# The bias of a Sin activation: a number in the instruction in place of a column in SBUF

## The chip, the cores and the metric

The kernel runs on one core of one Trainium2 chip. The metric is device microseconds of that core for one execution, and the median of a few runs is compared. The engines of the core are TensorE (PE in the profile, with its weight loads as PEld), VectorE (DVE), ScalarE (ACT), GpSimd (POOL) and SyncE (SP).

## The reference, cut to what matters

```python
# q, k, v: (4, 12480, 128); agents: (4, 49, 128); w_in: (128, 2048); w_out: (2048, 128), all fp32
def sm(a, b):                      # softmax of scaled scores over the last axis
    ...
a2k = sm(agents, k);  agent_v = a2k @ v          # 49 agents gather from 12480 keys
q2a = sm(q, agents);  x = (q2a @ agent_v).reshape(49920, 128)
h = x @ w_in                                      # 49920 x 2048
g = h * np.cos(h)
out = g @ w_out
```

Most of the arithmetic is the last three lines: for each of 49,920 tokens, 2,048 hidden values h, their cosine, and a second product.

## The kernel before, in words

**Tiling.** A batch has 13 groups of 960 tokens, so there are 52 groups. A group is worked in two halves of 480 tokens, and a half in 8 steps; a step handles 2 of the 16 blocks of 128 hidden units for 480 tokens. That makes 16 steps in a group and 832 in all. The projected agents times w_in are kept as `a`, so h comes straight from the softmax weights `pT` of the query: `ph = a' @ pT` (L520, two matmuls of 480 columns into a PSUM tile of two banks).

**A step.** After the two matmuls into `ph`, ScalarE computes cos(h) as Sin(h + pi/2) from `ph` into the SBUF tile `c` (L523), and VectorE computes r = (c - 1) * h from `c` and `ph` (L525). Four steps later TensorE multiplies r by w_out and accumulates into the PSUM tile `one` (L542). The missing "+ h" is added as two small matmuls at the end of each half (L538, L539). Then ScalarE copies the half's result from `one` to SBUF as `osb` (L544), and a DMA writes it out. `ph` has 3 buffers, `c` 3, `r` 6, and `one` 2: a step's matmuls into `ph` can start only when VectorE has read the `ph` of three steps earlier.

```python
cos = sb.tile([P, 2, CH], F32, name="c", bufs=3)
nc.scalar.activation(cos, h, AF.Sin, bias=half_pi, scale=1.0)
r = rs[n] = sb.tile([P, 2, CH], F32R, name="r", bufs=6)
nc.vector.scalar_tensor_tensor(r, cos, 1.0, h, op0=ALU.subtract, op1=ALU.mult)
```

**Work between the steps.** A plan written out by hand gives most steps one more piece of work: for the next batch, the agents' scores over the keys (L93 on TensorE, copied by ScalarE at L171), their exponentials (L214), and their product with v (L232); for the queries, scores (L93), maxima (L342), exponentials (L353), sums (L357) and weights, which TensorE turns (L372), ScalarE copies to SBUF as `p` (L374) and GpSimd splits into the rows of `pT` (L377, L378). The last batch has no next one, so from about 1000 us on only the steps, the `osb` copies and the turning of weights are left. Ahead of the steps, until about 85 us, the first batch's agents and the weights are prepared.

**Order.** The instructions of each engine stand in one queue and are executed in that order. The queues are written by a planner in the library: it takes instructions in the order of the program unless its own estimate of times says that a later one is ready sooner; exponentials are pinned to their place.

**The column.** `half_pi` is a tile of 128 x 1 fp32 in SBUF, filled with pi/2 by GpSimd at the start (L66). Sin reads it as bias at L523; a 1 x 1 Sin that brings the Sin table in early reads one element of it as its input (L386). A branch for large h (L564 on) has a Sin with the same bias (L625); it is executed only if the data ask for it. `HALF_PI` is the Python number.

Of the kernel before, what the change touches and what calls it, by code (L numbers as in the profile page):

```python
# [13 lines left out]
AF = mybir.ActivationFunctionType  # L14
# [12 lines left out]
HALF_PI = math.pi / 2  # L27
# [14 lines left out]
def agent_attention_cos_ffn(ctx, tc, qT, kT, v, agT, w_in, w_out, outT):  # L42
    nc = tc.nc
# [21 lines left out]
    half_pi = const.tile([P, 1], F32, name="half_pi")  # L65
# [21 lines left out]
    def scores(sb, src, b, ps):  # L87

        xt = sb.tile([P, GRP], F32, name="xt", bufs=3)
        load(xt, src)  # L90
        ps = ps[:TT, :GT * NA].rearrange("p (t a) -> p t a", a=NA)
        for t in range(GT):
            nc.tensor.matmul(ps[:, t, :], xt[:, t * TT:(t + 1) * TT], ag[:, b, :], start=True, stop=True)  # L93
        return ps
# [204 lines left out]
    with ExitStack() as pools:  # L299
# [4 lines left out]
        def small():  # L304
            return ps_1.tile([P, 512], F32, name="one")
# [206 lines left out]
        for n in range(NSTEP + LAG):  # L512
            pinned[0] = n < NP
            if n < NSTEP:
                q, c, i = n // STEP, n // NP % NCH, n % NP
                ai = a[q // NG % 2]
                ph = ps_h.tile([P, 2, 512], F32, name="ph")
                for j in range(2):
                    f = slice((2 * i + j) * P, (2 * i + j + 1) * P)
                    nc.tensor.matmul(ph[:, j, :CH], ai[:, f], pTs[q % 3][:, c], start=True, stop=True)  # L520
                h = ph[:, :, :CH]
                cos = sb.tile([P, 2, CH], F32, name="c", bufs=3)
                nc.scalar.activation(cos, h, AF.Sin, bias=half_pi, scale=1.0)  # L523
                r = rs[n] = sb.tile([P, 2, CH], F32R, name="r", bufs=6)
                nc.vector.scalar_tensor_tensor(r, cos, 1.0, h, op0=ALU.subtract, op1=ALU.mult)  # L525
            plan.run(n)
            m = n - LAG
            if m < 0:
                continue
            q, c, i = m // STEP, m // NP % NCH, m % NP  # L530
            if i == 0:
                if c == 0:
                    osb = sb.tile([P, GRP], F32, name="osb")
                po = small()[:, :CH]
            r = rs.pop(m)
            if i == NP - 1:
                k = q // NG % 2
                nc.tensor.matmul(po, b1[k], pTs[q % 3][:, c], start=False, stop=False)  # L538
                nc.tensor.matmul(po, b2[k], pTs[q % 3][:, c], start=False, stop=False)  # L539
            for j in range(2):  # L540
                f = 2 * i + j
                nc.tensor.matmul(po, w1[:, f, :], r[:, j, :], start=(f == 0), stop=(f == NF - 1))  # L542
            if i == NP - 1:
                nc.scalar.copy(osb[:, c * CH:(c + 1) * CH], po)  # L544
                at = q * GRP
                if q == NQ - 1:
                    nc.sync.dma_start(outT[:, at + c * CH:at + (c + 1) * CH], osb[:, c * CH:(c + 1) * CH])
                elif c == NCH - 1:
                    nc.sync.dma_start(outT[:, at:at + GRP], osb)
# [14 lines left out]
    with tc.If(far):  # L564
        with ExitStack() as pools:
# [19 lines left out]
            def group(b, src, dst):  # L585
                ps = scores(sb, src, b, small())
                mx = sb.tile([TT, GT], F32, name="mx2")
                nc.vector.reduce_max(mx, ps, axis=AX.X)
                e = sb.tile([TT, GT, NA], F32, name="e")
                nc.vector.tensor_sub(e, ps, mx.unsqueeze(2).to_broadcast([TT, GT, NA]))  # L590
                nc.scalar.activation(e, e, AF.Exp, scale=SC)
                rz = sb.tile([TT, GT], F32, name="rz2")
                nc.vector.reduce_sum(rz, e, axis=AX.X)
                nc.vector.tensor_scalar_add(rz, rz, EPS)
                nc.vector.reciprocal(rz, rz)
                nc.gpsimd.tensor_mul(p.rearrange("p t (h a) -> p h t a", h=2)[:, :, :, :NA],
                                     e.rearrange("p (h t) a -> p h t a", h=2),
                                     rz.rearrange("p (h t) -> p h t", h=2).unsqueeze(3).to_broadcast([TT, 2, HT, NA]))
                pt = small()
                for t in range(HT):  # L600
                    nc.tensor.transpose(pt[:KR, t * TT:(t + 1) * TT], p[:, t, :KR], ident[:TT, :TT])
                for c in range(NCH):
                    own, other = half_rows[c], half_rows[1 - c]
                    nc.scalar.copy(pT[own, c], pt[own, :CH])
                    nc.vector.tensor_sub(pT[other, c], pt[own, :CH], pT[own, c].bitcast(F32))
                osb = sb.tile([P, GRP], F32, name="osb")
                for c in range(NCH):
                    po = small()[:, :CH]
                    for i in range(NP):
                        ph = ps_h.tile([P, 2, 512], F32, name="ph")  # L610
                        for j in range(2):
                            f = slice((2 * i + j) * P, (2 * i + j + 1) * P)
                            nc.tensor.matmul(ph[:, j, :CH], a1[:, f], pT[:, c], start=True, stop=False)
                            nc.tensor.matmul(ph[:, j, :CH], a2[:, f], pT[:, c], start=False, stop=True)
                        h = ph[:, :, :CH]

                        k = sb.tile([P, 2, CH], F32, name="k", bufs=1)
                        nc.vector.tensor_scalar(k, h, 0.5 / math.pi, 0.25, op0=ALU.mult, op1=ALU.add)
                        nc.vector.tensor_scalar(k, k, ROUND, ROUND, op0=ALU.add, op1=ALU.subtract)
                        r = sb.tile([P, 2, CH], F32, name="r", bufs=1)  # L620
                        nc.vector.scalar_tensor_tensor(r, k, -TWO_PI_A, h, op0=ALU.mult, op1=ALU.add)
                        nc.vector.scalar_tensor_tensor(r, k, -TWO_PI_B, r, op0=ALU.mult, op1=ALU.add)
                        nc.vector.tensor_scalar(r, r, -4.7123885, 1.5707960, op0=ALU.max, op1=ALU.min)
                        cos = sb.tile([P, 2, CH], F32, name="c")
                        nc.scalar.activation(cos, r, AF.Sin, bias=half_pi, scale=1.0)  # L625
                        y = sb.tile([P, 2, CH], F32, name="g")
                        nc.vector.tensor_mul(y, h, cos)
                        g1 = sb.tile([P, 2, CH], F32R, name="g1")
                        nc.scalar.copy(g1, y)
                        g2 = sb.tile([P, 2, CH], F32R, name="g2")  # L630
                        nc.vector.tensor_sub(g2, y, g1.bitcast(F32))
                        for j in range(2):
                            f = 2 * i + j
                            nc.tensor.matmul(po, w1[:, f, :], g1[:, j, :], start=(f == 0), stop=False)
                            nc.tensor.matmul(po, w2[:, f, :], g1[:, j, :], start=False, stop=False)
                            nc.tensor.matmul(po, w1[:, f, :], g2[:, j, :], start=False, stop=(f == NF - 1))
                    nc.scalar.copy(osb[:, c * CH:(c + 1) * CH], po)
                nc.sync.dma_start(dst, osb)
# [55 lines left out]
```

## Time and profile before

| what | value |
|---|---|
| median of 3 runs | 1284.95 us (1282.61 to 1286.02) |
| span of the profiled execution | 1283.9 us |
| instructions | 17193 |
| granted TensorE clock, mean | 0.978 |
| PE, DVE, ACT, POOL busy | 93%, 85%, 78%, 24% |

The span runs from the first to the last instruction of one profiled execution, for which no other time of its own was taken. It is 1.05 us under the median of the runs, and within their spread. Shares of busy time are means over parts of the kernel that differ.

### The profile page before, as it was taken

The numbers are of one execution on the slowest core, as the hardware profiler recorded it, in microseconds if no ns is written. First come the engines' busy times: TensorE is split into PE (matmuls) and PEld (weight loads), VectorE is DVE, ScalarE is ACT, GpSimd is POOL, SyncE is SP. The second block draws the span as 40 slices with busy tenths as digits, with TensorE's granted clock in tenths as the row PEclk, the third lists the DMA queues.
The fourth block names the chain that finished last, engine by engine and source line by source line (L and its number), as shares of the span: only waits on it lengthen the run. The fifth ranks groups of instructions, "written<-read, shape, count | busy, mean of one in ns | idle before, by whom it ended". The sixth has DMA issues, their size and how long they took to land.

```text
span 1283.9 us, 17193 instructions
## 1 busy us (share of the span) xinstructions
PE 1188.2 (93%) x6349; PEld 955.3 (74%) x6349; DVE 1087.6 (85%) x1214; ACT 1005.6 (78%) x1115; POOL 313.8 (24%) x341
## 2 busy tenths in 40 slices
PE   8799899996999999969999999996999999999997
PEld 8777787775987887758966788775986666666664
DVE  5878778887779888878799988787789999999997
ACT  2347778667779887676799988667789999999997
POOL 1201221415213115133132121415133122222220
PEclk9989999998999999999999999998999999999999
DMA  8953333331440342324400133331500000000000
GB/s 301 247 153 111 92 108 108 93 109 61 109 108 31 108 131 70 108 77 108 133 22 31 54 116 93 108 93 31 136 19 32 31 16 31 31 31 16 31 31 34
DMA packets 31016, 107.72 MB, mean 84 GB/s; under 512 B 3436, under 2 KB 3820, under 8 KB 30924
## 3 DMA queue, kind: packets, MB, share of 16 engines
q1 hardware_dynamic: 30924, 106.54, 27.3%
q8 instruction: 52, 0.85, 0.3%
q14 instruction: 40, 0.33, 0.1%
HBM read 80.97 MB, written 25.56 MB: 83 GB/s over the span
## 4 chain that ended last, share of the span: by engine, by line
PE 56%; ACT 17%; DVE 15%; issue 7%; POOL 2%; DMA 2%; ACTq 0%; SPq 0%; POOLq 0%
PE ph L520 19%; PE one L542 14%; DVE r L525 13%; PE one L93 11%; ACT c L523 11%; PE one L232 5%; ACT osb L544 2%; PE ph L101 2%; DMA vt<-v 1%; PE ph L232 1%; PE one L538 1%; PE one L539 1%; DVE mx L342 1%; ACT e L353 1%; PE one L372 1%
## 5 line engine op out<-in xcount | busy, mean ns | idle before, releaser
L525 DVE SCALAR_TENSOR_TENSOR r<-c,ph 128x960 fp32r<-128x960 f32 x832 | 922.6, 1149 | 109.0 <-ACT c L523 104.2
L523 ACT ACTIVATE c<-ph,half_pi 128x960 f32<-128x960 f32 x832 | 859.3, 1068 | 198.6 <-PE ph L520 185.5
L520 PE MATMUL ph<-pT,a 113*128 113x480 f32 x1664 | 542.5, 407 | 33.2 <-DVE r L525 30.3
L542 PE MATMUL one<-r,w 128*128 128x480 f32 x1664 | 515.9, 389 | 3.9 <-ACT osb L544 2.8
L520 PEld LDWEIGHTS ph<-pT,a 113*128 113x128 f32 x1664 | 282.2, 190 | 167.6 <-DVE r L525 86.7
L542 PEld LDWEIGHTS one<-r,w 128*128 128x128 f32 x1664 | 308.1, 190 | 49.4 <-ACT osb L544 4.0
L363 POOL TENSOR_TENSOR p<-e,rz 120x392 f32<-120x392 f32 x52 | 44.9, 864 | 767.4 <-PE one L372 681.2
L93 PEld LDWEIGHTS one<-ag,xt 128*120 128x120 f32 x1408 | 164.1, 184 | 21.9 <-ACT osb L544 11.9
L93 PE MATMUL one<-ag,xt 128*120 128x49 f32 x1408 | 163.6, 265 | 2.5 <-ACT osb L544 0.6
L378 POOL TENSOR_TENSOR pT<-p,pT 49x480 fp32r<-49x480 f32 x104 | 127.1, 1222 | 8.0
L232 PE MATMUL one<-s,vt 120*128 120x98 f32 x624 | 80.6, 284 | 27.9 <-ACT osb L544 27.7
L232 PEld LDWEIGHTS one<-s,vt 120*128 120x128 f32 x624 | 80.2, 202 | 32.0 <-ACT osb L544 29.0
L377 POOL CAST pT<-p 49x480 fp32r<-49x480 f32 x104 | 61.4, 591 | 52.2 <-ACT p L374 48.9
L544 ACT COPY osb<-one 128x480 f32<-128x480 f32 x104 | 57.8, 556 | 2.7 <-PE one L542 2.7
L342 DVE TENSOR_REDUCE mx<-one 120x8 f32<-120x392 f32 x49 | 27.5, 562 | 32.2 <-PE one L93 32.2
L372 PEld LDWEIGHTS one<-ident,p 120*113 120x113 f32 x208 | 30.2, 179 | 22.3 <-ACT osb L544 16.5
L372 PE MATMUL one<-ident,p 120*113 120x120 f32 x208 | 37.3, 281 | 7.5 <-ACT osb L544 5.1
L538 PE MATMUL one<-pT,b 113*128 113x480 f32 x104 | 39.9, 383 | 0.0
L539 PE MATMUL one<-pT,b 113*128 113x480 f32 x104 | 39.8, 382 | 0.0
L357 DVE TENSOR_REDUCE rz<-e 120x32 f32<-120x1568 f32 (+2 forms) x12 | 22.7, 1916 | 18.2 <-ACT e L353 18.2
L210 POOL TENSOR_TENSOR s<-s,mxb 120x1568 f32<-120x1568 f32 (+1 forms) x9 | 31.4, 3522 | 26.9 <-DVE mxb L206 26.9
L222 POOL TENSOR_TENSOR es<-es,s 120x392 f32<-120x392 f32 x36 | 36.7, 1018 | 2.8
(91 smaller groups left out, 504.0 us busy)
## 6 DMA issues: line engine op xcount, KB each, us to landing
xt<-qT SPq DMA_DIRECT2D x52, 480.0 KB, 3.4
vt<-v SPq DMA_DIRECT2D x52, 480.0 KB, 4.3
outT<-osb SPq DMA_DIRECT2D x51, 480.0 KB, 2.5
xt<-kT SPq DMA_DIRECT2D x46, 480.0 KB, 3.5
c<-kT SPq DMA_DIRECT2D x6, 480.0 KB, 6.6
raw<-w_in SPq DMA_DIRECT2D x4, 512.0 KB, 5.7
raw<-w_out SPq DMA_DIRECT2D x4, 512.0 KB, 10.9
outT<-osb SPq DMA_DIRECT2D x2, 240.0 KB, 2.0
```

The source lines that it names most:

```text
L93: nc.tensor.matmul(ps[:, t, :], xt[:, t * TT:(t + 1) * TT], ag[:, b, :], start=True, stop=True)
L232: nc.tensor.matmul(po, vt[:, t, :], twice(e[:, t, :]), start=(t == 0 and (g == 0 or not lone)), stop=(t == GT - 1 and (g == NG - 1 or not ...
L372: nc.tensor.transpose(pt[:KR, t * TT:(t + 1) * TT], p_in[n % 2][:, t, :KR], ident[:TT, :TT])
L377: nc.gpsimd.tensor_copy(pT[own, c], p[own])
L378: nc.gpsimd.tensor_sub(pT[other, c], p[own], pT[own, c].bitcast(F32))
L520: nc.tensor.matmul(ph[:, j, :CH], ai[:, f], pTs[q % 3][:, c], start=True, stop=True)
L523: nc.scalar.activation(cos, h, AF.Sin, bias=half_pi, scale=1.0)
L525: nc.vector.scalar_tensor_tensor(r, cos, 1.0, h, op0=ALU.subtract, op1=ALU.mult)
L538: nc.tensor.matmul(po, b1[k], pTs[q % 3][:, c], start=False, stop=False)
L539: nc.tensor.matmul(po, b2[k], pTs[q % 3][:, c], start=False, stop=False)
L542: nc.tensor.matmul(po, w1[:, f, :], r[:, j, :], start=(f == 0), stop=(f == NF - 1))
L544: nc.scalar.copy(osb[:, c * CH:(c + 1) * CH], po)
```

## The change

At both places where a Sin has the column as its bias, the number pi/2 is given. The tile `half_pi`, its fill and the 1 x 1 Sin that reads it stay as they are.

```diff
                 cos = sb.tile([P, 2, CH], F32, name="c", bufs=3)
-                nc.scalar.activation(cos, h, AF.Sin, bias=half_pi, scale=1.0)
+                nc.scalar.activation(cos, h, AF.Sin, bias=HALF_PI, scale=1.0)
                 r = rs[n] = sb.tile([P, 2, CH], F32R, name="r", bufs=6)
...
                         cos = sb.tile([P, 2, CH], F32, name="c")
-                        nc.scalar.activation(cos, r, AF.Sin, bias=half_pi, scale=1.0)
+                        nc.scalar.activation(cos, r, AF.Sin, bias=HALF_PI, scale=1.0)
                         y = sb.tile([P, 2, CH], F32, name="g")
```

## Rows read from the trace of the kernel before

**Rows 1.** The page, part 1: busy us (share of the span) and instructions of each engine.

```profile
PE 1188.2 (93%) x6349; PEld 955.3 (74%) x6349; DVE 1087.6 (85%) x1214; ACT 1005.6 (78%) x1115; POOL 313.8 (24%) x341
```

**Rows 2.** Two stretches: their us, then each engine's busy us (and instructions), PEclk, DMA, GB/s.

```profile
85.00:1000.00 915.00, 852.77 (x4731) 701.36 (x4730) 762.63 (x850) 718.36 (x787) 241.41 (x249) 0.98 0.28 85
1000.00:1273.60 273.60, 260.47 (x1081) 185.14 (x1080) 263.06 (x242) 261.95 (x285) 59.93 (x68) 1.00 0.07 29
```

**Rows 3.** ScalarE, late stretch: timeline (start us, us, instruction xcount [idle before <-releaser]).

```profile
1159.19 1.07 ACT L523 ACTIVATE c<-ph,half_pi 128x960 f32<-128x960 f32 x1 [0.24 <-PE ph L520]
1160.15 0.55 ACT L544 COPY osb<-one 128x480 f32<-128x480 f32 x1
1160.59 7.32 ACT L523 ACTIVATE c<-ph,half_pi 128x960 f32<-128x960 f32 x7
1168.15 1.07 ACT L523 ACTIVATE c<-ph,half_pi 128x960 f32<-128x960 f32 x1 [0.25 <-PE ph L520]
1169.11 0.55 ACT L544 COPY osb<-one 128x480 f32<-128x480 f32 x1
1169.55 2.07 ACT L523 ACTIVATE c<-ph,half_pi 128x960 f32<-128x960 f32 x2
1171.52 0.55 ACT L374 COPY p<-one 113x480 f32<-113x480 f32 x1
1171.96 5.20 ACT L523 ACTIVATE c<-ph,half_pi 128x960 f32<-128x960 f32 x5
```

**Rows 4.** VectorE, the same stretch: timeline.

```profile
1161.69 8.71 DVE L525 SCALAR_TENSOR_TENSOR r<-c,ph 128x960 fp32r<-128x960 f32 x8 [0.25 <-ACT c L523]
1170.66 2.22 DVE L525 SCALAR_TENSOR_TENSOR r<-c,ph 128x960 fp32r<-128x960 f32 x2 [0.26 <-ACT c L523]
1173.07 5.41 DVE L525 SCALAR_TENSOR_TENSOR r<-c,ph 128x960 fp32r<-128x960 f32 x5 [0.18 <-ACT c L523]
```

**Rows 5.** Waits, 85 to 1000 us: who waited for whom, us in total, times, longest.

```profile
ACT c L523 <- PE ph L520: 179.4, 199, 2.8
DVE r L525 <- ACT c L523: 94.0, 136, 1.4
```

**Rows 6.** The chain that ended last, from 85 and from 1000 us on: shares by line.

```profile
by line: PE ph L520 20.1%; PE one L542 15.5%; PE one L93 15.2%; DVE r L525 11.8%; ACT c L523 8.1%; PE one L232 7.0%; issue 5.2%; ACT osb L544 2.6%; ACT e L353 1.5%; DVE mx L342 1.5%; PE one L372 1.4%; POOL es L222 1.4%; PE one L538 1.3%; PO
by line: ACT c L523 22.7%; DVE r L525 21.3%; PE ph L520 20.7%; issue 12.9%; PE one L542 12.2%; ACT osb L544 2.0%; PE one L538 2.0%; PE one L539 2.0%; ACT p L374 1.7%; ACTq L523 0.2%
```

**Rows 7.** ScalarE groups by line and shape: xcount, busy us, mean ns, idle before.

```profile
L523 ACT ACTIVATE c<-ph,half_pi 128x960 f32<-128x960 f32 x832 | 859.3, 1068 | 198.6 <-PE ph L520 185.5 <-DVE r L525 1.9 <-DVE mxb L206 1.3
L544 ACT COPY osb<-one 128x480 f32<-128x480 f32 x104 | 57.8, 556 | 2.7 <-PE one L542 2.7
L171 ACT COPY s<-one 120x392 f32<-120x392 f32 x39 | 19.0, 486 | 7.0 <-PE one L93 6.6
L266 ACT ACTIVATE a<-one,rz 113x512 fp32r<-113x512 f32 x16 | 11.2, 697 | 1.9 <-PE one L263 1.8
L353 ACT ACTIVATE e<-e 120x1960 f32<-120x1960 f32 x5 | 9.2, 1831 | 0.0
L353 ACT ACTIVATE e<-e 120x1568 f32<-120x1568 f32 x6 | 8.7, 1496 | 0.0
```

**Rows 8.** The chain that ended last: two Sins in a row, start us, us.

```profile
153.35 2.01 ACT c L523 x2
```

**Rows 9.** ScalarE's timeline from the first Sin to the first copy of `osb`.

```profile
85.52 2.96 ACT L523 ACTIVATE c<-ph,half_pi 128x960 f32<-128x960 f32 x3
88.35 0.39 ACT L277 ACTIVATE b<-one,rz 113x128 fp32r<-113x128 f32 x1
88.87 4.26 ACT L523 ACTIVATE c<-ph,half_pi 128x960 f32<-128x960 f32 x4
94.63 2.96 ACT L523 ACTIVATE c<-ph,half_pi 128x960 f32<-128x960 f32 x3 [1.50 <-PE ph L520]
99.15 1.06 ACT L523 ACTIVATE c<-ph,half_pi 128x960 f32<-128x960 f32 x1 [1.56 <-PE ph L520]
100.11 0.56 ACT L544 COPY osb<-one 128x480 f32<-128x480 f32 x1
```

**Rows 10.** TensorE's timeline before the copy of `osb` at 1160.15.

```profile
1158.99 0.60 PE L542 MATMUL one<-r,w 128*128 128x480 f32 x2
```

## The prediction

> **What bounds the kernel now.** I read the page first for the shares of each engine: TensorE is busiest, VectorE next, ScalarE third [rows 1]. None of them is full, so I asked the view by windows, and it falls into three parts. Until about 85 us no Sin runs, and the change can do nothing there. From 85 to 1000 us TensorE is busy 852.77 of 915 us (93%), VectorE 83% and ScalarE 79%: the steps share TensorE with the scores and the products with v. From 1000 to 1273.6 us, with only the steps left, VectorE is busy 263.06 and ScalarE 261.95 of 273.6 us, both 96% [rows 2].
>
> Busy time overstates a queue, because records overlap at their ends. So I read the pace from rows that hold several instructions: VectorE's five r's take 5.41 us with a last record of 1.15 us, so one starts every (5.41 - 1.15) / 4 = 1.065 us [rows 4]. Two Sins in a row take 2.01 us on the chain, and with the second's own 1.07 the first has 0.94 us to itself [rows 7, 8]. A group of 16 steps therefore needs 16 x 1.065 = 17.0 us of VectorE and 16 x 0.94 + 2 x 0.44 + 0.44 = 16.4 us of ScalarE (a copy is followed by its successor after 0.44 us, 1160.15 to 1160.59 [rows 3]). The late part has 242 steps in 273.6 us, or 18.1 us a group over 15.1 groups. VectorE is the slower queue, and some 1.1 us a group is lost to waits: 273.6 - 242 x 1.065 = 15.9 us in all.
>
> Where this is lost can be seen in one period of the timeline. Sin at 1159.19 is released by TensorE; the copy of `osb` follows at 1160.15, the next Sin at 1160.59 [rows 3], and the r that needs it starts at 1161.69 after VectorE sat idle for 0.25 us [rows 4]. In the second half the same happens (1168.15, 1169.11, 1169.55, r at 1170.66 after 0.26 us), and a copy of `p` at 1171.52 delays the Sin at 1171.96 and the r at 1173.07 by another 0.18 us [rows 3, 4]. So although ScalarE has the lighter load, each copy in its queue pushes a Sin past the moment at which VectorE wants it, and three `ph` buffers are too few to have a Sin in hand.
>
> In the part from 85 to 1000 us, VectorE waited for a Sin 136 times, 94.0 us in all, but the Sin itself waited for TensorE 199 times, 179.4 us [rows 5]. The chain that ended last puts 8.1% of that part on Sin, and 22.7% of the late part [rows 6].
>
> **The change, step by step.** It removes one operand of 832 Sins, the read of the column. It adds no instruction, wait or buffer. The column's fill, and the 1 x 1 Sin that reads it, stay. The second edit (L625) lies in the branch for large h, and the trace has no instruction of that line, so it costs nothing.
>
> *What one Sin saves.* A Sin of 960 elements takes 1068 ns. Rows without a column, read from PSUM like the Sin, are the copies: 556 ns at 480 elements and 486 at 392, so 70 ns for 88 elements, about 0.80 to 0.83 ns each; with 0.83, 158 ns stay above the elements. Activations with a column, from PSUM: 697 ns at 512 elements leaves 272, the Sin's 1068 - 797 leaves 271 [rows 7]. The difference is 0.11 us, the upper end; it still holds whatever separates an ACTIVATE from a COPY. The exponentials are ACTIVATEs without a column: 1831 - 1627 = 204 and 1496 - 1301 = 195 ns above their elements [rows 7], but read from SBUF, so 0.07 us is the lower end. I take 0.10 us, near the copies, because they read from PSUM as the Sin does. Nothing would be saved in pace if the column were read behind the Sin before it: the records overlap by 1.07 - 0.94 = 0.13 us. Even then the record, whose end VectorE waits for, would get shorter.
>
> The Trainium skill, "ScalarE: Activation LUTs", section "What ACT_TABLE_LOAD costs", puts a pointer operand at about 93 ns: 186 + 0.833 N ns with immediates against 280 + 0.833 N. For N = 960 it gives 1080 ns for the Sin as it is, and the trace has 1068 [rows 7]. By the page's 93 ns the sum below would be 10.2 us where mine is 11.0.
>
> *The late part.* In the first half of the period two Sins lie between TensorE's release and the late r: 1159.19 and 1160.59. Each is 0.10 us shorter, so r starts up to 0.2 us sooner, and its delay is 0.25 us of idle time plus the lost overlap. In the second half four lie in a row before the r at 1173.07 (1168.15, two from 1169.55, 1171.96): 0.4 us. Together 0.6 us a group, 15.1 x 0.6 = 9.1 us. It is an upper end: TensorE's release must not become the later one. The chain gives another count: 22.7% of 283.9 us is 64.4 us, or 60 Sins at 1.068; 60 x 0.10 = 6.0 us. I take the middle, 7.5 us.
>
> *The part from 85 to 1000 us.* 8.1% of 915 us is 74 us, 69 Sins, 6.9 us at most by the chain; the 136 waits give 13.6 us if each fell by the whole 0.10. Here TensorE comes right behind: where a Sin is released by TensorE's `ph`, its queue is full of scores, and an earlier r releases nothing that TensorE could take at once. I take half of the chain's count, 3.5 us; nothing at all is the other end.
>
> *What else moves.* ScalarE's queue gets 832 x 0.10 = 83 us lighter, but nearly all of it becomes idle time in front of the next Sin, which will wait more for TensorE or for a free buffer. What is late next: VectorE in the late part, at 17.0 us a group; TensorE before it.
>
> Sum: 7.5 + 3.5 = 11 us off the span of 1283.9, so 1272.9. The median of the runs lies 1.05 us above that span: **1274 us**.
>
> **The rivals.**
>
> *Hidden.* ScalarE is the third busiest engine, and what it gains is waited away: TensorE's 93% before 1000 us and VectorE's 96% after it set the time [rows 1, 2]. The time stays at 1285, give or take 3. For it: 179.4 us in which the Sin waited for TensorE [rows 5]. Against it: the late r's stand directly behind Sins [rows 4], and the chain runs through them [rows 6]. The Trainium skill, "Perfetto Trace Analysis", section "Identifying Performance Opportunities", has it that a kernel generally improves by its most-contended engine, the one with the highest occupancy; by that rule nothing would be gained. The chain of this trace doesn't bear it out for the late part. Here belongs too that the change does nothing, if the library puts the number into a column of its own: the Sin would keep 1068 ns. The exponentials, with a bias of zero, name no column [rows 7], which speaks against it.
>
> *The queues are written anew, and slower.* The planner moves instructions by its own times. The first copy of `osb` stands after 11 Sins (3 + 4 + 3 + 1) [rows 9], where the program has 12 before it, so it has been moved ahead of one. If it reckons with a shorter Sin, a copy can come one place earlier still. At the period shown the copy would take the place of the Sin at 1159.19, but its matmuls end at 1158.99 + 0.60 = 1159.59 [rows 10]: ScalarE would wait 0.40 us that it doesn't now, and VectorE behind it. Of 104 such copies, 27 make up for my 11 us; if half are moved the cost is 52 x 0.40 = 21 us, and the time 1274 + 21 = 1295. Against it: the copy now starts 0.56 us after its data are there, so a Sin shorter by 0.10 doesn't bring it there by itself.
>
> *More than forecast.* All of the late part's 9.1 us and all 136 waits before it, 22.7 us: 1262. It is the low end of my forecast.
>
> **How the numbers follow.** Forecast, a gain of 4 us (60 Sins at 0.07) to 22.7: 0.65, with its own range 1262 to 1281. Hidden: 0.21. Slower: 0.14. From no change this measurement can tell about 0.3%, 3.9 us, so faster means under 1281.1: 0.64, with the forecast's edge left out; same 0.22; slower 0.14. The range reaches from 1262, the low end, over the hidden case to 1287, and leaves out most of the slower case and little more.
>
> **What would show it.** The Sin's row names no `half_pi`, and its mean is 0.96 to 0.97 us. Two Sins in a row start 0.84 to 0.85 us apart. In the late part a group takes about 17.6 us where it took 18.1, the idle 0.25 us before r behind a copy falls under 0.1, and ScalarE waits more for TensorE. Before 1000 us TensorE's share goes up slightly, and VectorE's 94.0 us of waiting for Sins falls by 5 to 14 us. I am wrong if the Sin keeps its time (then nothing changes), if r still starts as late because TensorE's `ph` comes late, or if the order on ScalarE or TensorE differs and copies wait for matmuls.

## The result, and the profile after

The changed kernel takes 1269.54 us (median of 4 runs, 1268.44 to 1270.76) where the kernel before took 1285.49 beside it: a ratio of 0.9877, with a 95% interval of 0.9859 to 0.9895. That is 16 us less; 1274, or 11 us less, was predicted.

The page of the kernel after, part 1 and two groups of part 5 (busy us, mean ns of one | idle before, releaser):

```profile
PE 1182.8 (93%) x6349; PEld 957.7 (76%) x6349; DVE 1084.4 (86%) x1214; ACT 939.3 (74%) x1115; POOL 313.5 (25%) x341
L525 DVE SCALAR_TENSOR_TENSOR r<-c,ph 128x960 fp32r<-128x960 f32 x832 | 918.9, 1150 | 97.5 <-ACT c L523 96.0
L523 ACT ACTIVATE c<-ph 128x960 f32<-128x960 f32 x832 | 789.7, 978 | 249.5 <-PE ph L520 224.2
```

Sin no longer names the column and takes 978 ns instead of 1068 [rows 7]. ScalarE's busy time falls by 66 us, but the idle time before Sin rises from 198.6 to 249.5 us: most of what is saved is waited again, 39 us of it for TensorE (185.5 [rows 7] to 224.2). The span falls by 16.2 us. Waits of the kernel after, 85 to 1000 us:

```profile
ACT c L523 <- PE ph L520: 203.8, 238, 2.9
DVE r L525 <- ACT c L523: 88.9, 129, 1.2
```

Against [rows 5], ScalarE waits 24 us more for TensorE, VectorE 5 us less for Sin. The view by windows (us, then busy of PE, PEld, DVE, ACT, POOL with instructions, clock, DMA share, GB/s):

```profile
85.00:1000.00 915.00, 859.72 (x4767) 710.02 (x4766) 769.30 (x856) 677.73 (x794) 244.47 (x253) 0.98 0.29 85
1050.00:1250.00 200.00, 192.57 (x805) 138.47 (x804) 194.45 (x181) 181.41 (x214) 46.72 (x53) 1.00 0.07 28
```

TensorE's busy time up to 1000 us rises from 852.77 to 859.72 [rows 2], because more of the work fits into the same time: its 93% before was not a full engine. In the 200 us of the second line the kernel before gets through 177 r's, this one through 181. The line of before:

```profile
1050.00:1250.00 200.00, 190.15 (x793) 135.47 (x793) 192.12 (x177) 191.61 (x209) 46.75 (x53) 1.00 0.07 28
```

Of the 16.2 us between the two spans, 3.3 lie ahead of the first Sin (it starts at 85.5 and at 82.2 us). That is not the change's: in the profiles of this study, with the same instructions ahead of it, the first Sin starts anywhere from 79.0 to 85.5 us, under either order of the queues. From the first Sin to the last the profiles have 1188.1 us before and 1175.0 after, 13.1 us less. Timings below therefore go by the runs, or by stretches of the trace that begin with the first Sin or behind it.

### The profile page after: what moved, and what is told of

It is laid out like the page before. It is cut to its first block, busy times and chain, and to the rows that moved or that the text cites. A ratio compares the mean times of both kernels' runs of the same rounds, so it can differ in the third digit from the quotient of the medians.

```text
span 1267.7 us, 17196 instructions
## 1 busy us (share of the span) xinstructions
PE 1182.8 (93%) x6349; PEld 957.7 (76%) x6349; DVE 1084.4 (86%) x1214; ACT 939.3 (74%) x1115; POOL 313.5 (25%) x341
## 4 chain that ended last, share of the span: by engine, by line
PE 62%; DVE 19%; ACT 11%; issue 3%; POOL 3%; DMA 2%; ACTq 0%; SPq 0%; POOLq 0%; DVEq 0%
PE ph L520 23%; PE one L542 17%; DVE r L525 14%; PE one L93 10%; ACT c L523 7%; PE one L232 5%; ACT osb L544 2%; DMA raw<-w_out 1%; POOL es L222 1%; DVE mx L342 1%; PE one L372 1%; PE one L538 1%; PE one L539 1%; PE ph L232 1%; PE ph L101 1%
## 5 line engine op out<-in xcount | busy, mean ns | idle before, releaser
L523 ACT ACTIVATE c<-ph 128x960 f32<-128x960 f32 x832 | 789.7, 978 | 249.5 <-PE ph L520 224.2
L520 PEld LDWEIGHTS ph<-pT,a 113*128 113x128 f32 x1664 | 285.3, 190 | 156.8 <-DVE r L525 77.3
L93 PEld LDWEIGHTS one<-ag,xt 128*120 128x120 f32 x1408 | 163.9, 184 | 20.1 <-ACT osb L544 10.8
L357 DVE TENSOR_REDUCE rz<-e 120x32 f32<-120x1568 f32 (+2 forms) x12 | 22.7, 1916 | 17.7 <-ACT e L353 17.7
## 6 DMA issues: line engine op xcount, KB each, us to landing
raw<-w_out SPq DMA_DIRECT2D x4, 512.0 KB, 10.2
```

The costliest lines, as they stand in the source:

```text
L523: nc.scalar.activation(cos, h, AF.Sin, bias=HALF_PI, scale=1.0)
```

## The experiments

In all but one of these kernels the bias is swapped after the planner has written the queues, so that the length of Sin and the order of the queues can be set apart:

```diff
     with tile.TileContext(nc) as tc:
         agent_attention_cos_ffn(tc, *args)
+    for block in nc.main_func.blocks:
+        new = list(block.instructions)
+        for at, x in enumerate(new):
+            if <x is the Sin of a step, number `swapped`>:
+                if <condition of the experiment>:
+                    new[at] = copy.replace(x, ins=(x.ins[0],
+                        mybir.ImmediateValue(dtype=F32, value=HALF_PI), *x.ins[2:]))
+                swapped += 1
+        block.instructions = new
```

Where nothing else is said, this stands on the kernel before.

### The order and the bias apart

Condition `True`: the number with the order of before.

> All 832 Sins of the steps take the number, but every queue keeps the order of the kernel before; the swap is made after the planner has written the queues. Theory (the shorter Sin does it, the order is neutral): about the time of the changed kernel, 1267 to 1272 us, ratio to the kernel before 0.986 to 0.990. Rival (the planner's new order gives a good part of the gain): 1274 to 1279 us, which is what the prediction's 11 us by the Sin alone would make.

Measured: 1265.55 us, ratio 0.9844 (0.9818 to 0.9871). That is 1.5 us below the range of the theory, and far from the rival.

The reverse: the changed kernel, whose order of instructions differs on TensorE, ScalarE and VectorE and in three places on GpSimd, with the column put back (the Sin of the branch, which isn't executed, keeps its column too).

```diff
-    new[at] = copy.replace(x, ins=(x.ins[0], mybir.ImmediateValue(dtype=F32, value=HALF_PI), *x.ins[2:]))
+    new[at] = copy.replace(x, ins=(x.ins[0], column, *x.ins[2:]))     # column: half_pi, as in L523 before
```

> The queues of the changed kernel, but all 832 Sins of the steps read the column again. Theory (the shorter Sin does it): the time of the kernel before, 1283 to 1288 us, ratio 0.998 to 1.002, the Sin at 1068 ns. Rival (the new order gives 4 to 6 us): 1279 to 1282 us.

Measured: 1288.82 us, ratio 1.0029 (1.0011 to 1.0047), Sin at 1068 ns. So the shorter Sin makes the whole gain; the new order makes none, and with the column it costs 0.3%, a little more than was expected. To see whether it costs as much with the number, the changed kernel and the first experiment were run once more on one chip.

> The changed kernel once more, on one chip beside the kernel with the number in the old order. Theory (the planner's new order costs about 0.3%, as it does with the column): ratio to the kernel before 0.987 to 0.989, 1269 to 1272 us, and 3 to 5 us slower than the one in the old order. Rival (the two orders are the same with the number; the 4 us between them lay within the two intervals): both within 2 us of each other.

Measured: 1270.96 us, 0.9895 (0.9874 to 0.9916). This is the change itself once more, and 13 us less than the kernel before.

> The number in all 832 Sins, the queues in the order of the kernel before, once more. Theory: 0.984 to 0.986, 1264 to 1267 us. Rival (the orders are the same): 1267 to 1271, like the changed kernel.

Measured: 1268.03 us, 0.9868 (0.9847 to 0.9890). The old order is ahead both times, by 4.0 and by 2.9 us, but the intervals overlap, and the 1268.03 us lie in the range of the rival. Much of the scatter goes with the granted clock: at mean clocks of 0.971, 0.976 and 0.980 the runs of the new order took 1273.02, 1270.84 and 1268.29 us, those of the old one on the same chip 1269.53, 1269.18 and 1265.11, so at a like clock the old order is ahead each time. The traces settle it for the last 240 steps, where the granted clock is 1.00 in all of them. From the first of these Sins to the last one it takes 264.8 to 264.9 us with the number in the old order (three traces) and 266.2 in the new (two), 271.5 with the column in the old order (four) and 272.9 in the new (one): the new order costs 1.3 to 1.4 us there with either operand. The number in the old order is the fastest version of the study.

What costs it there can be read. TensorE in the late stretch of the changed kernel (start us, us):

```profile
1155.37 0.46 PE L372 MATMUL one<-ident,p 120*113 120x120 f32 x2 [0.19 <-ACT osb L544]
1155.59 0.68 PE L520 MATMUL ph<-pT,a 113*128 113x480 f32 x2
1156.11 0.60 PE L542 MATMUL one<-r,w 128*128 128x480 f32 x2
1156.55 0.37 PE L372 MATMUL one<-ident,p 120*113 120x120 f32 x2
```

And with the number in the old order:

```profile
1155.66 0.36 PE L372 MATMUL one<-ident,p 120*113 120x120 f32 x1 [0.19 <-ACT osb L544]
1155.78 0.67 PE L520 MATMUL ph<-pT,a 113*128 113x480 f32 x2
1156.30 0.60 PE L542 MATMUL one<-r,w 128*128 128x480 f32 x2
1156.74 0.47 PE L372 MATMUL one<-ident,p 120*113 120x120 f32 x3
```

The four turnings of weights are split 2 and 2 in place of 1 and 3, so the matmuls into `ph` start 0.22 instead of 0.12 us behind the first of them. VectorE's timeline of the changed kernel there:

```profile
1156.22 2.24 DVE L525 SCALAR_TENSOR_TENSOR r<-c,ph 128x960 fp32r<-128x960 f32 x2 [0.17 <-ACT c L523]
1158.64 6.48 DVE L525 SCALAR_TENSOR_TENSOR r<-c,ph 128x960 fp32r<-128x960 f32 x6 [0.17 <-ACT c L523]
```

And with the number in the old order:

```profile
1156.52 6.65 DVE L525 SCALAR_TENSOR_TENSOR r<-c,ph 128x960 fp32r<-128x960 f32 x6 [0.17 <-ACT c L523]
```

The new order has a second wait, at 1158.64, in each group; the old one runs through, and a group takes 17.74 us in place of 17.84. In the last 240 steps the turnings, in 14 groups, are all that stands in another place, so the 1.3 us there are theirs. Where the rest of the 3 to 4 us lies, ahead of these steps, isn't shown.

### The two parts

Conditions `swapped >= 592` and `swapped < 592`.

> The order of the kernel before; the number from step 592 on alone (the stretch from about 1000 us on), the column in the steps ahead of it. Prediction: 7.5 us off, 9.1 at the most: 1276 to 1280 us. The trace of the changed kernel has 5.5 us gained from step 592 to the end: 1279 to 1281. Rival (hidden behind VectorE): 1285.

Measured: 1277.15 us, 0.9937 (0.9913 to 0.9960).

> The order of the kernel before; the number in steps 0 to 591 alone. Prediction: 3.5 us off, 1281 to 1283 us. The trace of the changed kernel has 7 us gained between the first step and step 592, which would give 1277 to 1279; with the 3.5 us by which its first step came sooner as well, if these belong to the change, 1274 to 1276.

Measured: 1272.67 us, 0.9909 (0.9883 to 0.9934). The two reductions, 0.63% and 0.91%, add up to 1.54%; all 832 together gave 1.56%. The traces tell the same: duration and first and last start of Sin, in the kernel with the number late

```profile
L523 ACT ACTIVATE c<-ph,half_pi x592: 1050/1062/1134, 84.0 to 1000.1; 128x960 f32<-128x960 f32 x198
L523 ACT ACTIVATE c<-ph x240: 971/976/1007, 1001.2 to 1266.1; 128x960 f32<-128x960 f32 x120
```

and in the one with the number early:

```profile
L523 ACT ACTIVATE c<-ph x592: 957/972/1026, 80.8 to 986.1; 128x960 f32<-128x960 f32 x198
L523 ACT ACTIVATE c<-ph,half_pi x240: 1060/1065/1083, 987.2 to 1258.7; 128x960 f32<-128x960 f32 x120
```

The last 240 steps take 1266.1 - 1001.2 = 264.9 us with the number and 1258.7 - 987.2 = 271.5 with the column: 6.6 us, 0.44 a group. The first 592, up to the first Sin of the last 240, take 987.2 - 80.8 = 906.4 and 1001.2 - 84.0 = 917.2: 10.8 us. Against the trace of the kernel before, 1002.1 - 85.5 = 916.6, it is 10.2. So the early gain is about three times the predicted 3.5 us, and this run is faster than every range that was named for it; the late one lies in its range.

### A second column

```diff
+                    new[at] = copy.replace(x, ins=(x.ins[0], column, unit, x.ins[3]))     # unit: a column of ones as the scale
```

The column of ones is taken from the Sin of the branch, which gets it as its scale too.

> The order of the kernel before; each of the 832 Sins reads a second column in addition, of ones, as its scale, so the result is the same. One column less gained 20 us with this order. If time goes with the Sin's length (theory), a second column adds 0.09 to 0.11 us to each Sin (1.16 to 1.18 us) and 20 to 26 us to the kernel: 1305 to 1312. Rival (the column read by itself holds something up, and the second is read along with the first): the Sin stays at 1.07 us and the time at 1285.

Measured: 1306.46 us, 1.0160 (1.0136 to 1.0185), and Sin takes 1159 ns. One column more costs 91 ns and 1.6%, one less saves 90 ns and 1.6%: the time of the kernel follows the length of Sin evenly in both directions.

### Which Sins

Condition `swapped >= 592 and swapped % 16 in (2, 3, 4, 5, 10, 11)`: in the late part, the Sins directly before and after a copy.

> The order of the kernel before; the number only from step 592 on, and there only in the 6 of 16 Sins of a group that stand directly before or after a copy on ScalarE (step modulo 16 is 2, 3, 4, 5, 10 or 11): 90 Sins. Theory (the late part's loss lies at the copies, and these six stand in the chain): all of the gain that the number has there, 6 to 8 us: 1277 to 1280 us. Rival (it goes by the load of ScalarE, so each Sin counts alike): 6/16 of it, 2.5 to 3 us: 1282 to 1283.

Measured: 1277.53 us, 0.9940 (0.9922 to 0.9958): all of the late gain by 90 of 240 Sins. The other 150 (`not in`):

> As the run with the Sins beside copies, but the number in the other 10 of 16 Sins, 150 in all. Theory: next to nothing, 0 to 1 us: 1284 to 1286. Rival (each Sin counts alike): 10/16 of the late gain, 4 to 5 us: 1280 to 1282.

Measured: 1285.20 us, 1.0002 (0.9983 to 1.0021): nothing. ScalarE's timeline with the number beside copies:

```profile
1156.32 0.98 ACT L523 ACTIVATE c<-ph 128x960 f32<-128x960 f32 x1 [0.25 <-PE ph L520]
1157.19 0.55 ACT L544 COPY osb<-one 128x480 f32<-128x480 f32 x1
1157.63 0.99 ACT L523 ACTIVATE c<-ph 128x960 f32<-128x960 f32 x1
1158.49 6.36 ACT L523 ACTIVATE c<-ph,half_pi 128x960 f32<-128x960 f32 x6
```

VectorE's:

```profile
1158.65 8.61 DVE L525 SCALAR_TENSOR_TENSOR r<-c,ph 128x960 fp32r<-128x960 f32 x8 [0.17 <-ACT c L523]
1167.43 6.67 DVE L525 SCALAR_TENSOR_TENSOR r<-c,ph 128x960 fp32r<-128x960 f32 x6 [0.17 <-ACT c L523]
```

With the number between them, ScalarE:

```profile
1158.60 1.06 ACT L523 ACTIVATE c<-ph,half_pi 128x960 f32<-128x960 f32 x1 [0.34 <-PE ph L520]
1159.56 0.55 ACT L544 COPY osb<-one 128x480 f32<-128x480 f32 x1
1160.00 1.08 ACT L523 ACTIVATE c<-ph,half_pi 128x960 f32<-128x960 f32 x1
1160.95 1.84 ACT L523 ACTIVATE c<-ph 128x960 f32<-128x960 f32 x2
```

And VectorE:

```profile
1161.11 8.70 DVE L525 SCALAR_TENSOR_TENSOR r<-c,ph 128x960 fp32r<-128x960 f32 x8 [0.26 <-ACT c L523]
1170.06 2.22 DVE L525 SCALAR_TENSOR_TENSOR r<-c,ph 128x960 fp32r<-128x960 f32 x2 [0.26 <-ACT c L523]
1172.46 6.57 DVE L525 SCALAR_TENSOR_TENSOR r<-c,ph 128x960 fp32r<-128x960 f32 x6 [0.18 <-ACT c L523]
```

With the number between copies, VectorE keeps the three waits of [rows 4], although 10 of 16 Sins are shorter; those only wait longer for TensorE (0.34 us where it was 0.24 [rows 3]). With it beside them the waits fall to two of 0.17 us, and the trace of all Sins with the number looks the same.

The same cut in the steps 0 to 591, by the neighbours in ScalarE's queue: `swapped < 592 and <a neighbour is not a Sin>`, 314 Sins, and its opposite, 278.

> The order of the kernel before; the number only in steps 0 to 591, and there only in the Sins whose neighbour on ScalarE's queue is not a Sin (copies, exponentials, projections): some 310 of 592. Theory (there too the loss lies where a Sin is pushed by something else in the queue): most of the 9 to 12 us that all 592 give: 1274 to 1278. Rival (ahead of 1000 us any Sin that TensorE releases is in the chain): about half, 5 to 6 us: 1279 to 1281.

Measured: 1274.58 us, 0.9915 (0.9897 to 0.9934).

> The order of the kernel before; the number only in steps 0 to 591, and there only in the Sins whose two neighbours on ScalarE's queue are Sins: the rest of those 592. Theory (the loss lies where something else stands in the queue): 0 to 2 us off, 1283 to 1285. Rival (Sins that TensorE releases count too): the difference between all early Sins and those beside something else would be larger, 3 us or more: 1281 or less.

Measured: 1285.60 us, 1.0010 (0.9995 to 1.0025). Here too the Sins beside other work bring what all 592 bring (0.9909), within the intervals, and the rest brings nothing that the runs can show. The traces show a little of it: five groups with scores (steps 416 to 495) take 123.2 us before, 122.0 with the number in all early Sins, 122.4 with it in those beside other work and 122.8 with it in the rest; steps 48 to 127, with scores too, take 126.3, 125.1, 125.5 and 125.8. There some 0.45 of 1.2 us come from the rest.

## Why the prediction was right, and where its sizes were off

**What one Sin saves.** Taken at 0.10 us, it is 0.09: 1068 to 978 ns, and 1159 with two columns. The copies as an upper end (0.11) did hold something of their own, as was said. (The 0.83 ns for an element doesn't follow from the copies, 70 / 88 = 0.80; the activations with a column give it, (1068 - 697) / (960 - 512).) The Trainium skill, "ScalarE: Activation LUTs", section "What ACT_TABLE_LOAD costs", has 93 ns for a pointer operand; the 90 and 91 ns here agree with it better than my value. The pace falls along with the record: two of the shorter Sins in a row take 1.84 us, so, less the second's own 0.98, one starts 0.86 us after the other, where it was 0.94. The end at which the column is read behind the Sin before it is excluded.

**The late part.** Predicted 7.5 us between the hand count of 9.1 and the chain's 6.0; measured 6.6, nearer to the chain. The mechanism is as predicted, down to the six Sins of a group that carry it. In the changed kernel itself 271.5 - 266.2 = 5.3 us are left of it, since the new order takes 1.3. What was off is how it shows: the idle time behind a copy fell from 0.26 to 0.17 us, not under 0.1. From TensorE's release to the late r it was 1161.69 - 1159.19 = 2.50 us [rows 3, 4] and is 1158.65 - 1156.32 = 2.33, so two Sins were saved, as counted; but only half of it is idle time, and the other half is small losses among the r's that follow (8 of them in 8.61 us instead of 8.71). From one late r to the next the half with two Sins in the way takes 1170.66 - 1161.69 = 8.97 us before and 1167.43 - 1158.65 = 8.78 with the number beside copies, 0.19 us of the 0.2 counted. The half with four Sins has the other 0.25 of the 0.44 us a group, where 0.4 were counted: its wait behind the copy of `p` was 0.18 us [rows 4] and is gone, and the rest of the 0.4 found no wait to shorten.

**85 to 1000 us.** This term failed: "I take half of the chain's count, 3.5 us", because TensorE's queue was full of scores and an earlier r would release nothing that it could take at once. Measured 10.2 to 10.8 us in the traces, and 0.91% of the time, which is 11.7 us (8.5 to 15.0 by the interval): more than the whole chain's 6.9 and not much under the 13.6 of all waits. The wrong step is that TensorE was taken to have no room; its 93% over 915 us was read as a full engine. The view by windows of before, for a stretch of steps with hardly anything else, one with scores and one with the products with v:

```profile
657.00:731.00 74.00, 70.74 (x308) 51.58 (x307) 70.74 (x69) 70.22 (x79) 18.86 (x22) 1.00 0.09 33
742.00:856.00 114.00, 109.81 (x647) 91.23 (x645) 94.70 (x106) 86.52 (x98) 32.60 (x28) 1.00 0.33 101
585.00:646.00 61.00, 60.59 (x368) 53.70 (x367) 48.12 (x58) 44.01 (x49) 9.08 (x11) 1.00 0.45 122
```

TensorE is busy 96% in the first two and 99% in the third. By the starts of the Sins, in the traces of before and of the number early, four groups in the first (steps 352 to 415) take 74.7 and 73.0 us, five groups with scores (416 to 495) 123.2 and 122.0, and a group with the products (320 to 335) 24.2 and 24.2. So the scores didn't keep TensorE full either; only the products did. All stretches like the first (steps 176 to 207 and 560 to 591 as well) give 3.4 us, all with scores (48 to 127 and 208 to 287 as well) 3.6. The other 3 us of the 10.2 lie in the first 48 steps and around the products, where traces of the same instructions differ by as much, and aren't put down to a cause here. From 657 to 731 us the trace of before has VectorE like this:

```profile
706.57 8.71 DVE L525 SCALAR_TENSOR_TENSOR r<-c,ph 128x960 fp32r<-128x960 f32 x8 [0.26 <-ACT c L523]
715.53 2.22 DVE L525 SCALAR_TENSOR_TENSOR r<-c,ph 128x960 fp32r<-128x960 f32 x2 [0.26 <-ACT c L523]
717.93 4.35 DVE L525 SCALAR_TENSOR_TENSOR r<-c,ph 128x960 fp32r<-128x960 f32 x4 [0.18 <-ACT c L523]
```

These are the waits of [rows 4], within 0.01 us. The chain by line, from 657 to 731 us and from 585 to 646 us of before, where the products with v fill TensorE:

```profile
by line: PE ph L520 28.0%; ACT c L523 18.0%; PE one L542 17.1%; DVE r L525 13.8%; issue 11.5%; PE one L93 2.3%; ACT osb L544 2.3%; PE one L539 2.1%; PE one L538 2.1%; DVE big L268 1.6%; ACT p L374 1.4%; PE one L372 0.6%; ACTq L523 0.2%
by line: PE one L232 32.2%; PE one L542 29.0%; PE ph L520 28.8%; DVE r L525 3.6%; PE one L372 1.9%; PE one L539 1.8%; PE one L538 1.8%; PE one L263 1.4%; DVE av L237 0.3%; PE one L249 0.2%; issue 0.1%
```

Sin holds 18.0% of the one and none of the other; from 730 to 853.3 us, with scores, it holds 7.6%. A row for each stretch would have told the cover from the place where there is none. In the first of them TensorE itself, by its weight loads, waited for r 26 times, 9.6 us in all.

**The sum.** That 1274 came near is in part luck: the early term was too small by some 7 us, the late one too large by 1, and the new order, which the forecast put at nothing, took 3 to 4 off again. That makes 13 us, as the repeated run of the change had it; the first had 16. The range of 1262 to 1287 also holds a kernel that gains nothing, so the measured time lying in it says little; that the shorter Sin did it is shown by the experiments.

**The rivals.** *Hidden*: nearly true of 428 of the 832 Sins, those with Sins on both sides, and false of the kernel. The Trainium skill, "Perfetto Trace Analysis", section "Identifying Performance Opportunities", would have the most-contended engine improved; ScalarE was behind VectorE by busy share (78% and 85% [rows 1]), and shortening its Sin by 8% gave 1.2%, so this trace doesn't bear the rule out. *New order*: it did happen and it costs, though not by copies that wait for their matmuls: in the traces of both kernels each of the 104 copies of `osb` follows the same Sin. It costs 0.3% with the column, and in the late part it is the turning of weights. Its price was put at 21 us, and was 3 to 4.

**What else was to show.** TensorE's share up to 1000 us rose, VectorE's wait for Sin fell by 5.1 us (5 to 14 were named), and a group of the late part takes 264.9 / 239 x 16 = 17.7 us with the number in the old order, 266.2 / 239 x 16 = 17.8 in the changed kernel (17.6 were named) and 271.5 / 239 x 16 = 18.2 with the column.

## What to carry to other kernels

An engine with idle time can still set the pace, at the places where a different instruction in its queue pushes the one that the next engine waits for; here shortening the instructions next to it brought nearly the whole gain, and the rest next to nothing. Read a cover from each stretch by itself, with who waits for whom, since a busy share over 900 us mixes stretches that are full with others that are not; and of this kernel's stretches those with TensorE 96% busy still had time to gain, the one with 99% had none. Where a planner orders the queues by its own times, a shorter instruction also gives another order; swapping the operand after the order is written keeps the two apart.

## What the runs showed of the hardware

A bias given as a number instead of a column takes 90 ns off an activation of 128 x 960 from PSUM, and a scale given as a column adds 91 ns to it (978, 1068 and 1159 ns). The time from the start of the span to the first Sin differs by up to 6.5 us between profiled executions whose instructions up to there are the same. The granted clock up to there was 1.00 where it came at 79.0 us and 0.92 where it came at 85.5, but 0.94 with 80.4 us and 0.96 with 84.0, so the clock alone doesn't explain it, and the cause stays open.
